# Block-wise weight conversions, a later half normalisation and a moved transpose in a fused attention and MoE kernel

## The chip, the cores and the metric

The kernel runs on one core of one Trainium2 chip. The metric is the device time of one execution in microseconds; the time of a kernel is the median of its runs. A core has TensorE (PE in the rows; PEld is its weight load), VectorE (DVE), ScalarE (ACT), GpSimd (POOL), and SyncE (SP), which in this kernel only issues transfers (DMAs). Each engine works through its own queue in order; an instruction that waits holds up all that is queued behind it on its engine.

## What is computed

The inputs are fp32. Attention with 2 x 8 heads, 768 tokens and 64 numbers a token is masked by clusters: a query sees the keys whose nearest of 16 centroids is the same. Two expert layers follow.

```python
def _attn_ref(q, k, v, centroids):
    ...
    q_assign = np.argmax(np.einsum('bhsd,hcd->bhsc', q_n, c_n), axis=-1)
    k_assign = np.argmax(np.einsum('bhsd,hcd->bhsc', k_n, c_n), axis=-1)
    mask = q_assign[:, :, :, None] == k_assign[:, :, None, :]
    scores = scale * np.matmul(q, k.transpose(0, 1, 3, 2))
    scores = np.where(mask, scores, -1000000000.0)
    ...
    return np.matmul(attn, v).astype(np.float32)

def _moe_ref(x, w_in, w_out):
    h = x @ w_in
    r = np.maximum(h, 0.0)
    return ((r * r) @ w_out).astype(np.float32)

def _moe2_ref(x, domain_probs, w1, w2):
    ...
    for e in range(E):
        h = np.maximum(x @ w1[e], 0.0)
        out += p[:, e:e + 1] * (h @ w2[e])
```

## The kernel before

All products run on fp32 numbers split in two parts, an upper one that TensorE's fp32r format holds and the rest (names with h and l: nkh, nkl, pth, ptl, w0h, w0l). The kernel has two stages. The attention stage takes the first quarter of the time; the two expert layers, a long row of products on TensorE, take the rest.

**Turns.** The attention stage is a loop over g = 0 to 95, one turn for each of 16 heads x 6 blocks of 128 queries. The work of a block is spread over turns. In turn g TensorE makes the scores S of block g + 2 (line 604, four products) and the transposes T of the exponentials of block g (line 637, six); VectorE makes the row maximum nb of block g + 2 (line 613); ScalarE the exponential p of block g + 1 (line 624); ScalarE and VectorE take T out of PSUM as pth (line 642) and ptl (line 643); the products with v (lines 651 and 653) follow for an earlier pair of blocks. The tables ORDER (one for even, one for odd turns) set in which order the code for a turn's steps is written, and so each engine's queue. A letter is a step: S, M (maximum), E (exponential), T0 and T1, P0 and P1 (products with v), O (taking their result out, line 675), and room for other work: X1 and X2 are two slots, each of which takes one function from the list `slots` for that turn, with its evacuation at Y1 or Y2; R runs the list `early`; C takes one step from the list dq; K is the place of the weight conversions.

**Pairs.** Heads go in pairs, 12 turns each. "Place p" below is turn g with g mod 12 = p. For the next pair of heads these steps are laid into a pair's turns:

- places 10, 11, 0, 1: the transposes of k and q (`trans_slot`, line 369, four slots). ScalarE takes each out as kqf (line 376), and GpSimd makes the upper parts nkh, nqh (line 52, `round_pool`) and the rests nkl, nql (line 378);
- places 1 and 2: the assignment scores (`pair_scores`, line 419), two halves, from nkh, nkl, nqh, nql; ScalarE copies them to ys (line 425);
- places 2 and 3: the scores are transposed back (`pair_turn`, line 435), two halves of three transposes; VectorE reduces each (line 440). All these steps share one PSUM buffer m;
- places 4 to 7: the one-hot rows. VectorE's maxima (lines 476, 480) and GpSimd's lines 465 to 473 are taken from dq; at place 7 TensorE transposes the result (`pair_hot`, line 492), and SyncE spreads it (`hot_rows`, line 509);
- `stack`: SyncE copies nkh, nkl, nqh, nql into the operands k1, q1, k2, q2 of the scores (lines 390, 392), for one head at places 1 and 3, for the other at places 8 and 9. GpSimd may write the next pair's nkh when these copies have landed.

Two more loads lie in these turns. `norm_steps` divides a finished pair's result by its row sums: the reciprocal (lines 707, 708) at place 3, its transpose (line 713) at place 4, a transfer through HBM that spreads it into rb (line 725) at place 5, a sum (line 734) at place 6, and then on GpSimd the two halves f5(0) and f5(1) at places 7 and 8: a product into rb (line 688), its upper part (line 52) and the rest (line 697), into xa. And `split64` converts the first layer's first weights, four blocks, which arrive as 64-bit words, to fp32: f1, f2, f4, f5, f6 on VectorE (lines 167, 170, 173, 178, 183), all in one buffer cva, then f3: ScalarE's copy w0h (line 189) and GpSimd's subtraction w0l (line 191), which reads cva last. They form one list cq of 24 steps; from turn 8 on a turn at places 6 to 10 takes one step, the blocks following each other without regard to the places. `load_piece` brings pieces of the next weights by SyncE, two at place 10 when the list is short enough.

Of the kernel before, what the change touches and what calls it, by code (L numbers as in the profile page):

```python
# [28 lines left out]
AT = {"stack1": (-11, -10), "stack": (-9, -9), "ohd": -7, "splitv": -3, "load": -10,  # L29
      "t": [-14, -13, -12, -11], "a": [-11, -10, -10, -9, -5], "conv": 8, "turns": (6, 7, 8, 9, 10)}  # L30


@with_exitstack
def moe_attention_kernel(
# [19 lines left out]
    B, H, S, D = q.shape  # L54
# [151 lines left out]
    with tc.manual_schedule():  # L206
# [175 lines left out]
        def stack(i, part):  # L382
            (kh, kl), (qh, ql) = kq[i // 2, "nk"], kq[i // 2, "nq"]
            r = slice(D * (i % 2), D * (i % 2) + D)
            for nm, rows, top, low in ((("k1", 128, kh, kl),),
                                       (("q1", 128, qh, qh), ("k2", D + C, kh, None),
                                        ("q2", D + C, ql, None)))[part]:
                t = stk[i, nm] = stk_p.tile(
                    [rows, S], F32R, tag=nm, name=nm, bufs=3 if nm == "k1" else 2)
                nc.sync.dma_start(out=t[0:D].bitcast(F32), in_=top[r].bitcast(F32))  # L390
                if low is not None:
                    nc.sync.dma_start(out=t[D:2 * D].bitcast(F32), in_=low[r].bitcast(F32))
# [307 lines left out]
        def norm_steps(hp):  # L700
# [38 lines left out]

            return [[f1], [], [f2], [f3], [f4], [lambda: f5(0)], [lambda: f5(1)]]  # L740

# [382 lines left out]
        for j in range(1, NH // 2):  # L1124
# [3 lines left out]
            for n, f in enumerate([pair_scores(j, 0), pair_scores(j, 1), pair_turn(j, 0),  # L1128
                                   pair_turn(j, 1), pair_hot(j)]):
                u = START["a"][n] if j == 1 else u0 + AT["a"][n]  # L1130
                if n == 4:
                    at(slots, u, lambda: None)
# [4 lines left out]
        for kk in range(KD):  # L1137
            at(early, 2 * NTT + kk, lambda kk=kk: load_in(kk))
        cq, lq = [], []
        for j in range(NF):  # L1140
            cq += [f for fs in split64(0, 0, j, cv_p[0]) for f in fs]
        for half in range(2):
            lq += [lambda half=half, n=n: load_piece(half, n) for n in range(4)]
        nq = []
# [5 lines left out]
        for g in range(NU):  # L1150
# [31 lines left out]
            def convert():  # L1182
                turn = g % (2 * NTT)
                if g >= AT["conv"] and cq and not dq and turn in AT["turns"]:
                    cq.pop(0)()
                if lq and turn == AT["turns"][-1] and len(cq) <= (12 if len(lq) > 4 else 0):
                    for _ in range(2):
                        lq.pop(0)()

# [202 lines left out]
```

## Time and profile before

| | |
|---|---|
| time of the kernel, median of 3 runs | 1040.4 us (1039.88 to 1041.51) |
| the profiled execution's own time | 1040.2 us |
| its span, first to last instruction | 1038.4 us |
| TensorE busy | 1016.5 us (98%) |
| VectorE, ScalarE, GpSimd busy | 676.1, 528.8, 567.5 us |

The profile is one execution, with a row for each instruction. Starts are counted from the first instruction. The granted clock is the share of TensorE's full 2.4 GHz. Idle time of an engine before an instruction is shown in square brackets with what ended it; an arrow in a wait reads "waited for".

### The profile page before, as it was taken

Reading aid. Unit: us, or ns where it says so; the run is one execution under the profiler, and the core shown is the slowest. Engines: PE = TensorE matmul, PEld = TensorE weight load, DVE = VectorE, ACT = ScalarE, POOL = GpSimd, SP = SyncE. Lnnn points to the kernel's source line nnn. Section 1 sums busy time; section 2 is a strip of 40 time slices with the busy share of each in tenths; the row PEclk is TensorE's granted clock in tenths of the full one; section 3 lists DMA queues with packets and bytes.
Section 4 is the critical chain, followed back from the end, with each engine's and each line's share of the span. In section 5 each row is a group of like instructions: output and inputs, shape, how many; then the busy total and the mean of one; then the engine's idle time right before and its main releaser. Section 6 shows DMA issues by size and latency. Waiting matters only on the chain.

```text
span 1038.4 us, 14897 instructions
## 1 busy us (share of the span) xinstructions
PE 1016.5 (98%) x5507; PEld 901.7 (87%) x5507; DVE 676.1 (65%) x1047; ACT 528.8 (51%) x1066; POOL 567.5 (55%) x557
## 2 busy tenths in 40 slices
PE   8998999999999999999999999999999999999998
PEld 7987888989888888888888998998988888898897
DVE  8887898879786773741175555577776555555654
ACT  7886887889755443434343333333444333333331
POOL 4465766665332222235456566567678566576650
PEclk9999999999999999999999999999999999999999
DMA  6576666665023230221012122122123121121101
GB/s 149 123 178 149 147 162 144 155 164 128 1 83 121 82 118 5 84 78 41 1 41 82 41 81 81 41 82 76 47 81 126 57 81 61 62 82 56 67 1 62
DMA packets 73745, 88.86 MB, mean 86 GB/s; under 512 B 27252, under 2 KB 50184, under 8 KB 73672
## 3 DMA queue, kind: packets, MB, share of 16 engines
q1 hardware_dynamic: 73672, 87.91, 29.8%
q8 instruction: 43, 0.70, 0.3%
q14 instruction: 30, 0.25, 0.1%
HBM read 62.58 MB, written 3.19 MB: 63 GB/s over the span
## 4 chain that ended last, share of the span: by engine, by line
PE 81%; DVE 3%; DMA 1%; SPq 1%; ACT 1%; POOL 1%; issue 1%; POOLq 0%; ACTq 0%
PE bank L965 25%; PE bank L925 22%; PE bank L818 13%; PE bank L794 4%; PE bank L793 4%; PE bank L795 4%; PE t L637 2%; PE s L604 2%; PE po L651 1%; PE po L653 1%; DVE ptl L643 1%; DVE nb L613 1%; PE m L419 1%; PE s L793 0%; DMA k<-nkh 0%
## 5 line engine op out<-in xcount | busy, mean ns | idle before, releaser
L965 PE MATMUL bank<-w1h,ga 128*128 128x512 f32 x768 | 269.9, 393 | 0.0
L975 DVE SCALAR_TENSOR_TENSOR x<-bank,pe_p,x 128x512 f32<-128x512 f32 x180 | 134.8, 750 | 167.5 <-PE bank L965 167.4
L925 PE MATMUL bank<-xa,w0h 128*128 128x384 f32 x896 | 228.2, 335 | 0.1
L925 PEld LDWEIGHTS bank<-xa,w0h 128*128 128x128 f32 x896 | 164.5, 188 | 17.9 <-ACT fa L936 0.5
L965 PEld LDWEIGHTS bank<-w1h,ga 128*128 128x128 f32 x768 | 144.1, 188 | 24.5
L804 POOL TENSOR_TENSOR ga<-fa,ga 128x512 fp32r<-128x512 f32 x48 | 63.2, 1317 | 178.0 <-ACT ga L803 137.0
L965 PE MATMUL bank<-w1l,ga 128*128 128x512 f32 x384 | 151.6, 395 | 0.0
L925 PE MATMUL bank<-xa,w0l 128*128 128x384 f32 x448 | 149.7, 334 | 0.0
L936 ACT COPY fa<-bank 128x384 f32<-128x384 f32 x96 | 45.6, 475 | 171.6 <-PE bank L925 171.6
L818 PE MATMUL bank<-ga,w1h 128*128 128x512 f32 x384 | 126.6, 389 | 0.0
L945 ACT ACTIVATE ga<-fa 128x384 fp32r<-128x384 f32 x96 | 50.5, 526 | 135.5 <-DVE fa L939 135.5
L894 POOL TENSOR_TENSOR w0l<-raw,w0h 128x512 fp32r<-128x512 f32 x64 | 75.0, 1195 | 81.2 <-ACT w0h L893 81.2
L912 POOL TENSOR_TENSOR w1l<-raw,w1h 128x1024 fp32r<-128x1024 f32 x32 | 77.2, 2414 | 71.3 <-ACT w1h L911 71.3
L643 DVE TENSOR_TENSOR ptl<-t,pth 128x384 fp32r<-128x384 f32 x192 | 97.7, 547 | 21.3 <-ACT pth L642 20.6
L613 DVE TENSOR_REDUCE nb<-s 128x1 f32<-128x768 f32 x96 | 91.2, 950 | 16.3 <-PE s L604 15.0
L637 PE MATMUL t<-identf,p 128*128 128x128 f32 x576 | 87.5, 279 | 7.7 <-DVE ptl L643 7.6
L624 ACT ACTIVATE p<-s,nb 128x768 f32<-128x768 f32 x96 | 88.0, 917 | 9.0 <-DVE nb L613 8.7
L642 ACT CAST pth<-t 128x384 fp32r<-128x384 f32 x192 | 84.0, 486 | 14.5 <-PE t L637 14.4
L948 DVE SCALAR_TENSOR_TENSOR ga<-fa,ga 128x384 fp32r<-128x384 f32 x96 | 90.1, 938 | 0.6 <-ACT ga L945 0.6
L604 PE MATMUL s<-k,q 80*128 80x384 f32 (+1 forms) x384 | 85.2, 343 | 0.5 <-DMA k<-ohm 0.3
L801 ACT ACTIVATE fa<-bank 128x512 f32<-128x512 f32 x44 | 26.4, 599 | 116.3 <-PE bank L795 116.3
L818 PEld LDWEIGHTS bank<-ga,w1h 128*128 128x128 f32 x384 | 72.0, 188 | 14.8
(213 smaller groups left out, 2051.9 us busy)
## 6 DMA issues: line engine op xcount, KB each, us to landing
raw<-in_moe_w_dram SPq DMA_DIRECT2D x64, 512.0 KB, 4.4
raw<-in_moe_w_in_dram SPq DMA_DIRECT2D x7, 1024.0 KB, 5.2
raw<-in_moe_w_out_dram SPq DMA_DIRECT2D x6, 1024.0 KB, 4.8
k<-nkh SPq DMA_DIRECT2D x28, 192.0 KB, 3.5
q<-nqh SPq DMA_DIRECT2D x28, 192.0 KB, 4.0
nv<-in_v_dram SPq DMA_DIRECT2D x16, 192.0 KB, 3.8
out_dram<-x SPq DMA_DIRECT2D x12, 256.0 KB, 2.1
k<-nkl SPq DMA_DIRECT2D x14, 192.0 KB, 3.3
```

Source lines behind the costliest of these rows:

```text
L604: nc.tensor.matmul(s[:, j, 0:HALF], stk[i, nq][:, t * 128:(t + 1) * 128], stk[i, nk][:, j * HALF:(j + 1) * HALF], start=first, stop=not first)
L613: nc.vector.tensor_reduce(out=nb, in_=s_ps[u][:, :, 0:HALF], axis=AX.XY, op=ALU.max, negate=True)
L624: nc.scalar.activation(p, s_ps.pop(u)[:, :, 0:HALF], AF.Exp, bias=nb_t.pop(u), accum_out=sums_t[hp][:, i % 2, t:t + 1])
L637: nc.tensor.transpose(tp[:, j], p_sb[u][:, half, j * 128:(j + 1) * 128], identf)
L642: return (lambda: nc.scalar.copy(dh, tp), lambda: nc.vector.tensor_tensor(dl, tp, dh.bitcast(F32), op=ALU.subtract))
L643: lambda: nc.vector.tensor_tensor(dl, tp, dh.bitcast(F32), op=ALU.subtract))
L818: nc.tensor.matmul(o, a, b, start=(ft == 0 and z == 0), stop=(ft == NF - 1 and z == 2))
L912: nc.gpsimd.tensor_tensor(lo, w, hi.bitcast(F32), op=ALU.subtract)
L925: nc.tensor.matmul(ps, w[:, o:o + 128], r_op(r, x)[:, kt], start=(first and kt == 0 and z == 0), stop=(kt == 1 and z == 2), skip_group_che ...
L948: nc.vector.scalar_tensor_tensor(out=g_t(n, f, t, 1), in0=h_src(n, f, t), scalar=0.0, in1=g_t(n, f, t, 0).bitcast(F32), op0=ALU.max, op1=A ...
L965: nc.tensor.matmul(o, a, w[:, f], start=(f == 0 and z == 0), stop=(f == 1 and z == 2))
L975: nc.vector.scalar_tensor_tensor(out=acc, in0=o, scalar=pc, in1=acc, op0=ALU.mult, op1=ALU.add)
```

## The change

Four things are laid out anew; no instruction is added or left out. The conversion steps get turns of their own: the first block 8, 9, 10, 18, 19 and, for f3, 27; block j = 1 to 3 the places 6 to 10 of one pair and place 3 of the next for f3 (turns 30 to 34 and 39, and so on). The load pieces stand at turns 46, 58, 70 and 82 (before: 34, 46, 70 and 82). f5(1) leaves place 8 and stands at place 2, in the next pair's turns; for the last but one pair it stays. The second `pair_turn` of each pair but the first goes to the second slot of its turn, behind the products with v. And `stack` copies k2 before q1.

```diff
--- before.py
+++ after.py
@@ -27,7 +27,7 @@
 WARM = [12, 10, 5, 11, 3, 9]
 START = {'t': [0, 0, 1, 1], 'a': [3, 3, 4, 4, 7], 'stack1': 4, 'stack': 5, 'head': 2}
 AT = {"stack1": (-11, -10), "stack": (-9, -9), "ohd": -7, "splitv": -3, "load": -10,
-      "t": [-14, -13, -12, -11], "a": [-11, -10, -10, -9, -5], "conv": 8, "turns": (6, 7, 8, 9, 10)}
+      "t": [-14, -13, -12, -11], "a": [-11, -10, -10, -9, -5], "conv": (8, 9, 10, 18, 19, 27), "pieces": 46, "second": 2}
 
 
 @with_exitstack
@@ -383,7 +383,7 @@
             (kh, kl), (qh, ql) = kq[i // 2, "nk"], kq[i // 2, "nq"]
             r = slice(D * (i % 2), D * (i % 2) + D)
             for nm, rows, top, low in ((("k1", 128, kh, kl),),
-                                       (("q1", 128, qh, qh), ("k2", D + C, kh, None),
+                                       (("k2", D + C, kh, None), ("q1", 128, qh, qh),
                                         ("q2", D + C, ql, None)))[part]:
                 t = stk[i, nm] = stk_p.tile(
                     [rows, S], F32R, tag=nm, name=nm, bufs=3 if nm == "k1" else 2)
@@ -737,7 +737,10 @@
             def f5(half):
                 norm_scaled(hp, half, st["rb"][:, half * HALF:(half + 1) * HALF], nc.gpsimd, round_pool)
 
-            return [[f1], [], [f2], [f3], [f4], [lambda: f5(0)], [lambda: f5(1)]]
+            if hp == NH // 2 - 2:
+                return [[f1], [], [f2], [f3], [f4], [lambda: f5(0)], [lambda: f5(1)]]
+            at(early, (2 * hp + 4) * NTT + AT["second"], lambda: f5(1))
+            return [[f1], [], [f2], [f3], [f4], [lambda: f5(0)]]
 
         def norm_last(hp):
             st = {}
@@ -1128,7 +1131,7 @@
             for n, f in enumerate([pair_scores(j, 0), pair_scores(j, 1), pair_turn(j, 0),
                                    pair_turn(j, 1), pair_hot(j)]):
                 u = START["a"][n] if j == 1 else u0 + AT["a"][n]
-                if n == 4:
+                if n == 4 or n == 3 and j > 1:
                     at(slots, u, lambda: None)
                 at(slots, u, f)
             if j + 1 < NH // 2:
@@ -1136,11 +1139,15 @@
         at(slots, START["head"], onehot_slot(1))
         for kk in range(KD):
             at(early, 2 * NTT + kk, lambda kk=kk: load_in(kk))
-        cq, lq = [], []
+        convs = {}
         for j in range(NF):
-            cq += [f for fs in split64(0, 0, j, cv_p[0]) for f in fs]
-        for half in range(2):
-            lq += [lambda half=half, n=n: load_piece(half, n) for n in range(4)]
+            steps = [f for fs in split64(0, 0, j, cv_p[0]) for f in fs]
+            b0 = (2 * j + 3) * NTT
+            turns = AT["conv"] if j == 0 else [b0 + x for x in (0, 1, 2, 3, 4, 9)]
+            for u, f in zip(turns, steps):
+                at(convs, u, f)
+        for n in range(8):
+            at(convs, AT["pieces"] + n // 2 * 2 * NTT, lambda n=n: load_piece(n // 4, n % 4))
         nq = []
 
         def early_gemm1(n):
@@ -1180,12 +1187,8 @@
                     f()
 
             def convert():
-                turn = g % (2 * NTT)
-                if g >= AT["conv"] and cq and not dq and turn in AT["turns"]:
-                    cq.pop(0)()
-                if lq and turn == AT["turns"][-1] and len(cq) <= (12 if len(lq) > 4 else 0):
-                    for _ in range(2):
-                        lq.pop(0)()
+                for f in convs.pop(g, []):
+                    f()
 
             def finish(n):
                 f = end.pop(n, None)
```

How the queues change, at three places. GpSimd, from the end of f5(0) on, in the turns 45 to 51 (nk and nq are the next pair's k and q, vv the split of v). Before:

```order
L688 TENSOR_TENSOR rb<-rb,xs 128x384
L52 TENSOR_SCALAR xa<-rb 128x128
L697 TENSOR_TENSOR xa<-rb,xa 128x128
L52 TENSOR_SCALAR xa<-rb 128x256
L697 TENSOR_TENSOR xa<-rb,xa 128x256
L52 TENSOR_SCALAR vv<-nv 128x6x64
L310 TENSOR_TENSOR vv<-nv,vv 128x6x64
L52 TENSOR_SCALAR nkh<-kqf 128x384
L378 TENSOR_TENSOR nkl<-kqf,nkh 128x384
L191 TENSOR_TENSOR w0l<-cva,w0h 128x4x128
L52 TENSOR_SCALAR nkh<-kqf 128x384
L378 TENSOR_TENSOR nkl<-kqf,nkh 128x384
```

After, from the last rounding of q on; the rows from vv to this one now follow f5(0) directly:

```order
L52 TENSOR_SCALAR nqh<-kqf 128x384
L378 TENSOR_TENSOR nql<-kqf,nqh 128x384
L688 TENSOR_TENSOR rb<-rb,xs 128x384
L52 TENSOR_SCALAR xa<-rb 128x128
L697 TENSOR_TENSOR xa<-rb,xa 128x128
L52 TENSOR_SCALAR xa<-rb 128x256
L697 TENSOR_TENSOR xa<-rb,xa 128x256
L52 TENSOR_SCALAR vv<-nv 128x6x64
L310 TENSOR_TENSOR vv<-nv,vv 128x6x64
L191 TENSOR_TENSOR w0l<-cva,w0h 128x4x128
```

The five rows of f5(1) stood ahead of the rounding of k and q and now stand behind it; line 191 stood between two of the roundings and now follows all of them.

VectorE at places 2 to 4 of the pair from turn 12 on. Before:

```order
L440 TENSOR_REDUCE A<-m 128x192
L613 TENSOR_REDUCE nb<-s 128x1
L440 TENSOR_REDUCE A<-m 128x192
L707 TENSOR_SCALAR r<-sums 128x12
L643 TENSOR_TENSOR ptl<-t,pth 128x3x128
L708 RECIPROCAL r<-r 128x12
L643 TENSOR_TENSOR ptl<-t,pth 128x3x128
L613 TENSOR_REDUCE nb<-s 128x1
L476 TENSOR_REDUCE mx<-A 128x24
```

After:

```order
L440 TENSOR_REDUCE A<-m 128x192
L613 TENSOR_REDUCE nb<-s 128x1
L707 TENSOR_SCALAR r<-sums 128x12
L643 TENSOR_TENSOR ptl<-t,pth 128x3x128
L708 RECIPROCAL r<-r 128x12
L643 TENSOR_TENSOR ptl<-t,pth 128x3x128
L440 TENSOR_REDUCE A<-m 128x192
L613 TENSOR_REDUCE nb<-s 128x1
L476 TENSOR_REDUCE mx<-A 128x24
```

The second reduction (line 440) moved from ahead of the reciprocal and of both ptl to behind them, just ahead of the next row maximum.

SyncE, the copies into the score operands of one head (k_762 is k1; k_808 before and k_805 after are k2; q_805 before and q_807 after are q1; q_810 is q2). Before:

```order
L390 DMA k_762<-nkh 64x768
L392 DMA k_762<-nkl 64x768
L390 DMA q_805<-nqh 64x768
L392 DMA q_805<-nqh 64x768
L390 DMA k_808<-nkh 64x768
L390 DMA q_810<-nql 64x768
```

After:

```order
L390 DMA k_762<-nkh 64x768
L392 DMA k_762<-nkl 64x768
L390 DMA k_805<-nkh 64x768
L390 DMA q_807<-nqh 64x768
L392 DMA q_807<-nqh 64x768
L390 DMA q_810<-nql 64x768
```

The copy into k2, the last one that reads nkh, moved ahead of the two copies into q1.

## Rows read from the trace of the kernel before

**Rows 1.** The page: the chain of work that ended last, by engine.

```profile
PE 81%; DVE 3%; DMA 1%; SPq 1%; ACT 1%; POOL 1%; issue 1%; POOLq 0%; ACTq 0%
```

**Rows 2.** Stretches: us; busy PE, PEld, DVE, ACT, POOL; granted clock; DMA share; GB/s.

```profile
42.05:59.18 17.13, 16.16 (x121) 15.06 (x120) 12.52 (x22) 14.16 (x35) 7.49 (x10) 1.00 0.70 169
73.17:95.33 22.16, 17.30 (x121) 16.38 (x120) 13.65 (x22) 14.92 (x36) 15.80 (x21) 0.92 0.50 113
109.35:127.67 18.32, 16.47 (x122) 14.85 (x120) 13.61 (x22) 15.04 (x36) 15.55 (x21) 1.00 0.68 157
141.68:162.37 20.69, 18.18 (x122) 16.43 (x120) 13.88 (x23) 15.35 (x37) 16.14 (x21) 0.92 0.67 158
176.01:193.23 17.22, 16.25 (x122) 14.91 (x120) 14.49 (x23) 14.37 (x35) 14.21 (x20) 1.00 0.63 139
207.22:224.40 17.18, 16.21 (x122) 15.08 (x120) 11.71 (x19) 14.19 (x35) 14.39 (x21) 1.00 0.72 169
207.22:216.74 9.52, 9.52 (x76) 9.07 (x75) 7.64 (x12) 8.91 (x23) 7.39 (x12) 1.00 0.76 162
89.18:95.33 6.15, 6.15 (x48) 6.05 (x47) 4.06 (x7) 5.29 (x14) 4.34 (x6) 1.00 0.18 35
```

**Rows 3.** Waits, 20 to 290 us: total us, times, longest us.

```profile
DVE cva L167 <- POOL w0l L191: 6.9, 2, 5.4
...
PE m L419 <- POOL nqh L52: 2.2, 3, 1.6
...
POOL A L465 <- DVE mx L476: 39.6, 7, 6.9
```

**Rows 4.** Timeline of pass 2: start, us, engine, line, operation, [idle before].

```profile
77.58 1.02 POOL L688 TENSOR_TENSOR rb<-rb,xs 128x384 f32<-128x384 f32 x1
...
80.66 1.26 POOL L191 TENSOR_TENSOR w0l<-cva,w0h 128x512 fp32r<-128x512 f32 x1
...
81.96 0.72 DVE L167 TENSOR_SCALAR cva<-raw 128x512 int32<-128x512 int32 x1 [5.36 <-POOL w0l L191]
...
84.06 1.54 PE L637 MATMUL t<-identf,p 128*128 128x128 f32 x6 [4.51 <-DVE ptl L643]
```

**Rows 5.** Timelines, line 183 beside GpSimd; line 189: ns min/median/max.

```profile
145.48 0.67 DVE L183 SCALAR_TENSOR_TENSOR cva<-raw,cva 128x512 int32<-128x512 int32 x1
...
182.35 1.42 DVE L183 SCALAR_TENSOR_TENSOR cva<-raw,cva 128x512 int32<-128x512 int32 x1
...
182.22 1.01 POOL L310 TENSOR_TENSOR vv<-nv,vv 128x384 fp32r<-128x384 f32 x1
...
L189 ACT CAST w0h<-cva x10: 614/632/661, 73.5 to 423.9; 128x512 fp32r<-128x512 f32 x10
```

**Rows 6.** Timeline of pass 4, SyncE (SPq), GpSimd; last: us to landing.

```profile
144.90 0.57 SPq L390 DMA_DIRECT2D q<-nqh  x1
...
146.51 0.87 SPq L390 DMA_DIRECT2D k<-nkh  x1
...
151.44 0.51 POOL L52 TENSOR_SCALAR nkh<-kqf 128x384 fp32r<-128x384 f32 x1 [1.81 <-ACT p L624]
...
k<-nkh SPq DMA_DIRECT2D x2, 192.0 KB, 4.7
```

**Rows 7.** Place 3 (turn 39) as a stretch; timeline of turns 39 to 41.

```profile
127.67:130.76 3.09, 2.70 (x22) 2.38 (x21) 3.02 (x7) 1.88 (x5) 0.00 (x0) 1.00 1.01 240
...
128.41 0.55 DVE L440 TENSOR_REDUCE A<-m 128x192 f32<-128x384 f32 x1
...
129.00 0.31 PEld L435 LDWEIGHTS m<-identf,ys 128*128 128x128 f32 x3 [0.71 <-DVE A L440]
...
131.68 0.96 DVE L613 TENSOR_REDUCE nb<-s 128x1 f32<-128x768 f32 x1
...
133.01 1.01 DVE L643 TENSOR_TENSOR ptl<-t,pth 128x384 fp32r<-128x384 f32 x2
...
133.65 0.97 PE L637 MATMUL t<-identf,p 128*128 128x128 f32 x6
```

## The prediction

> **What bounds the kernel now.** I read the chain of work that ended last first: TensorE carries 81% of it, the other engines a few per cent in all [rows 1]. From 286 us on that is TensorE without a gap, and the change does not reach there. So the question is how much TensorE loses in the attention stage, and I cut that stage by turns, whose starts are the first score product on line 604 of each. A pair of heads is 12 turns; I write "place 9" for the tenth turn of a pair. The work for the next pair (its transposes, its assignment scores) lies at places 10, 11, 0, 1 and 2, so I took the stretches of places 9 to 2. There are six; I call them passes 1 to 6, in order of time. Two undisturbed pieces give the length that TensorE needs: places 9 to 0 of pass 6, 9.52 us, and places 1 and 2 of pass 2, 6.15 us. In both TensorE is busy all the time, so 15.67 us is the floor. Against it the six passes are too long by 1.46, 6.49, 2.65, 5.02, 1.55 and 1.51 us, together 18.7 us [rows 2]. That is all that this change can take from these stretches.
>
> The list of waits of the attention stage says what ends them [rows 3]: VectorE's first conversion step (line 167, writing cva) waited 6.9 us in two places for GpSimd's line 191, the last reader of cva; TensorE's assignment scores (line 419) waited 2.2 us in three places for GpSimd's rounding of q (line 52). GpSimd itself stood idle 39.6 us in seven places before line 465. It is late in one part of the pair and idle in another.
>
> **The conversions.** The timeline of pass 2 shows the largest loss whole [rows 4]. GpSimd starts the second half of the normalisation (line 688) at 77.58, comes to line 191 at 80.66 and leaves it at 81.92; VectorE, which had taken up line 167 of the next block, has stood 5.36 us; the row maximum and the exponential behind it are late, and TensorE idles 4.51 us before its transposes. What is queued behind line 167 on VectorE is thus every turn's work. TensorE's clock falls with it: passes 2 and 4, in which TensorE is idle longest (4.9 and 2.5 us), have a mean granted clock of 0.92, so for a part of them the lower of its two levels, 1.2 instead of 2.4 GHz; the other four have 1.00 [rows 2]. This loss is inside the 6.49 and 5.02 us and goes with the idling.
>
> After the change a block's five VectorE steps stand at places 6 to 10 and the ScalarE copy with line 191 at place 3 behind them, three turns (over 6 us) ahead of the next block's line 167. That wait has no place left. What stays is VectorE's own load: five steps in five turns. Pass 5 has exactly this layout today (turns 54 to 58), so its 1.55 us is the upper bound for passes 3, 4 and 5; the lower is 0, pass 6, which has no steps. In between: pass 5's last step (line 183) took 1.42 us, since GpSimd was in line 310; not held up, it took 0.67 in pass 4 [rows 5]. With the second half of the normalisation gone from there, GpSimd runs line 310 some 2.9 us earlier, is through with it and waits for a DMA when that step comes. I take 0.75 us off and leave 0.8 us in each of passes 3, 4 and 5, and 0.5 in pass 2, where only two of the block's steps (turns 18 and 19) precede. The copy on ScalarE (line 189) stands at the end of place 3, where ScalarE is busy 1.88 of 3.09 us [rows 7]: nothing. If that cover were gone it would cost its own length, 0.63 us [rows 5], four times.
>
> That GpSimd and VectorE block each other is also what the Trainium skill states ("SBUF — State Buffer", Who interferes with whom): a VectorE instruction in a 2-port mode, or with two SBUF inputs, and a GpSimd instruction hold a shared port pair in turn. By that rule the moved GpSimd work could hit VectorE at places 2 and 3; this is the third rival below.
>
> **The half normalisation.** In each pair 2.9 us of GpSimd work (77.58 to 80.7 in pass 2, [rows 4]) leave the queue ahead of the rounding of k and q and go behind it, to place 2. Five or three instructions move; they issue no DMA. In passes 2 to 6 the rounding is ready earlier. Behind them now wait the value split and line 191, and then line 465. The idle time before line 465 is 39.6/7 = 5.7 us a pair; 2.9 + 1.3 us of moved work leave 1.5 us. So I cost it at nothing. The transfer that reads the normalised buffer's successor (rb, line 725) is issued at place 5, and ScalarE's first copy into the same xs buffer comes at the end of place 3, a full turn after the place where line 688 reads it.
>
> **k2 first on SyncE's queue.** GpSimd may overwrite nkh only when its last reader, the transfer into k2 (line 390), has landed. In pass 4 that one was issued at 146.51, two transfers after 144.90, and GpSimd began at 151.44, when it had landed (4.7 us) [rows 6]. Now it is issued in the place of the first q1 transfer, 1.6 us earlier. Passes 1 and 6 are too long by 1.46 and 1.51 us and wait for nothing else, so both go to 0; in passes 3 to 5 it helps too. Bounds: 0 to 1.6 us a pass. q1 lands later by one transfer; its reader is seven turns away.
>
> The Trainium skill says that completion on such a queue is not in order of issue ("DMA: Bandwidth & Descriptors", Queues, rings and completion order). By that k2 could land as late as now, and the sum would be that of the second rival. The row, 4.7 us from issue to landing, does not decide it alone.
>
> Pass by pass the excess after is then 0, 0.5, 0.8, 0.8, 0.8 and 0: 2.9 us of 18.7 stay, **15.8 us go**.
>
> **The second transposes back.** At place 3 the three transposes of line 435 waited for VectorE to clear the one buffer m, and TensorE stood 0.71 us before their weight load [rows 7]. Behind the products of the turn they wait for nothing. So six pairs could gain up to 6 x 0.7 = 4.3 us. But VectorE has no slack: from 128.41 it works without a break to the row maximum at 131.68, which waits 0.2 us, and then to the two line 643 at 133.01; TensorE's transposes, which write into what the first of them has read, start at 133.65 [rows 7]. TensorE that comes 0.7 us earlier meets the same VectorE, and gains the 0.2 us. It can lose too: the reciprocal's transpose (line 713) in the next turn uses m, and now waits for line 440, so below nothing by one line 440, 0.55 us, or -3.3 us. Between -3.3 and 4.3 I take 0.2 x 6 less 0.4 us that turn 51 loses because it no longer profits from the stall before it: **0.8 us**.
>
> The load pieces move to turns 46, 58, 70 and 82, the last two as now; what they bring is converted only after the attention stage. Nothing.
>
> **Sum.** Own time of the profiled execution 1040.2 us (span 1038.4 and 1.8 around it; the median of the three runs is 1040.4). 1040.2 - 15.8 - 0.8 = **1023.6 us**.
>
> **Rivals.** (1) The transposes give their full 0.7 us, because VectorE's chain is shorter than I think: 0.8 becomes 4.3, **1020.1 us**. For it: TensorE's wait there is real; against it: VectorE's unbroken row of work. (2) The k2 transfer lands no earlier, or GpSimd is late anyway: passes 1, 4 and 6 keep 1.5 us each, **1028.1 us**. For it: transfers there crowd (DMA share 0.67 to 0.72 in those stretches, [rows 2]); against: the start at 151.44 follows the landing at once. (3) The moved GpSimd work blocks VectorE's small SBUF steps at place 3 (lines 707 and 708): up to one GpSimd instruction, 1.0 us, in each of six pairs, and the 0.8 us are lost: **1030.4 us**. Against it: line 707 ran in places with an idle GpSimd, so no row shows it; and by my order of events GpSimd is at that moment waiting for line 189. (4) On the other side: GpSimd becomes late for the one-hot rows, which it makes in lines 465 to 473 and which TensorE transposes at place 7 (line 492). It decides from the point where the moved work ends more than 1.5 us later than I reckon; each further us is then one of TensorE's in each of six pairs, since all of its later work is queued behind line 492. Slower by 0.2% needs a loss of 16.6 + 2.1 us, with a little over it 3.2 us a pair, so a GpSimd that is 4.7 us late: the moved 4.2 us would have to take twice as long. That gives 1023.6 + 6 x 3.2 = **1042.8 us**. (5) All goes back into VectorE's load and nothing is left, within 0.2% (about what a measurement of this kernel can tell from no change): the 5.36 us wait cannot come back, so this is very unlikely.
>
> **How the numbers follow.** Forecast 0.72, rivals (1) 0.09, (2) 0.09, (3) 0.06, (4) 0.02, (5) 0.02. The range takes in (1) and (2), and the bounds of VectorE's load, 3 x 0.75 us up, 3 x 0.8 and 0.5 down: 1019.0 to 1029.0 us. Faster 0.96, same 0.02, slower 0.02.
>
> **What will show it.** In the changed profile: no wait of line 167 for line 191; no wait of line 419 for GpSimd; granted clock 1.00 in all six passes; each pass between 15.6 and 16.5 us; line 435 without idle time, place 3 shorter but places 4 and 5 longer by most of it; GpSimd's idle time before line 465 down to 1 or 2 us a pair. I would be wrong if line 465 no longer waits for VectorE, if GpSimd's first nkh still begins some 5 us after the q1 issue, or if passes 3 and 4 stay above 17 us.

## The result, and the profile after

The changed kernel takes 1025.9 us (median of 4 runs, 1025.34 to 1028.38) against 1040.14 for the kernel before beside it (4 runs): a ratio of 0.9866, with a 95% interval of 0.9847 to 0.9884. Forecast were 1023.6 us and a range of 1019.0 to 1029.0. The profiled execution took 1025.7 us (span 1023.7; before 1040.2 and 1038.4). The slowest of the four runs, 1028.38 us, had a mean granted clock of 0.998 over its span, the other three 0.999 to 1.000.

The chain of work that ended last [rows 1] can't be compared. In the kernel before it is followed back only to 119.7 us, in the changed kernel to 0.7 us, so TensorE's 81% there and 86% here are shares of different stretches.

The six passes, cut as in [rows 2] (stretch; us; busy PE, PEld, DVE, ACT, POOL; granted clock; DMA share; GB/s):

```profile
43.08:58.75 15.67, 15.67 (x122) 15.14 (x120) 12.54 (x22) 14.17 (x35) 7.47 (x10) 1.00 0.69 163
72.36:89.85 17.49, 16.03 (x122) 15.05 (x120) 12.31 (x20) 14.31 (x35) 11.95 (x17) 1.00 0.69 159
103.82:120.09 16.27, 15.89 (x121) 14.98 (x120) 13.17 (x23) 14.23 (x35) 12.11 (x17) 1.00 0.66 144
134.27:150.62 16.35, 16.29 (x122) 14.89 (x120) 13.79 (x23) 14.28 (x35) 11.50 (x16) 1.00 0.75 178
164.86:180.53 15.67, 15.67 (x121) 14.99 (x120) 13.12 (x23) 14.21 (x35) 12.54 (x18) 1.00 0.76 179
194.22:210.15 15.93, 15.91 (x122) 15.08 (x120) 11.71 (x19) 14.24 (x35) 12.27 (x18) 1.00 0.71 170
```

Over the floor of 15.67 us they are too long by 0, 1.82, 0.60, 0.68, 0 and 0.26 us, together 3.4. Forecast were 0, 0.5, 0.8, 0.8, 0.8 and 0, together 2.9. The granted clock is 1.00 in all six. So the passes gave 15.3 us where 15.8 were forecast, and one of them, the second, is off by 1.3 us.

Places 3 to 5, where the moved transposes lie, are to be read pair by pair (turns 15 to 17, 27 to 29, and so on; same columns):

```profile
58.75:65.85 7.10, 7.04 (x55) 6.51 (x54) 7.10 (x15) 5.96 (x15) 1.83 (x3) 1.00 1.09 224
89.85:97.31 7.46, 7.04 (x55) 6.48 (x54) 7.46 (x15) 6.49 (x16) 5.49 (x8) 1.00 1.02 231
120.09:127.76 7.67, 7.21 (x55) 6.45 (x54) 7.67 (x15) 6.49 (x16) 5.71 (x9) 1.00 0.93 215
150.62:158.37 7.75, 7.26 (x56) 6.45 (x54) 7.75 (x15) 6.49 (x16) 5.78 (x9) 1.00 1.09 235
180.53:187.71 7.18, 7.04 (x55) 6.49 (x54) 7.18 (x15) 6.43 (x16) 5.29 (x7) 1.00 1.16 221
210.15:217.25 7.10, 7.04 (x55) 6.52 (x54) 7.10 (x15) 5.96 (x15) 3.91 (x6) 1.00 0.95 223
```

Before, these stretches took 7.49, 7.51, 7.51, 7.13, 7.49 and 7.51 us (from the same starts of line 604). VectorE is busy for the whole of each, as [rows 7] had it. The first and the last pair fell to 7.10 us; of the four between, two fell (7.18 and 7.46) and two are longer than before (7.67 and 7.75). In all it is 0.4 us, forecast 0.8.

The list of waits of the attention stage (20 to 290 us; total us, times, longest) answers [rows 3]:

```profile
POOL A L465 <- DVE mx L476: 15.3, 7, 5.8
POOL rb L688 <- DMA rb<-rd: 15.0, 6, 4.5
...
PEld m L713 <- DVE A L440: 3.0, 6, 0.7
...
PE s L604 <- DMA k<-ohm: 1.5, 2, 1.1
...
PE m L713 <- DVE A L440: 1.3, 3, 0.5
```

Line 167's wait for line 191 (6.9 us before) and TensorE's line 419 waiting for line 52 (2.2) are gone from the list. GpSimd's idle time before line 465 fell from 39.6 to 15.3 us. TensorE's wait of line 604 for the one-hot rows (k<-ohm) grew from 0.3 us in one place to 1.5 in two, and its wait of line 713 for line 440 is new.

### The profile page after: what moved, and what is told of

Read it like the earlier page. It is cut to its first block, busy times and chain, and to the rows that moved or that the text cites. A ratio compares the mean times of both kernels' runs of the same rounds, so it can differ in the third digit from the quotient of the medians.

```text
span 1023.7 us, 14890 instructions
## 1 busy us (share of the span) xinstructions
PE 1012.1 (99%) x5507; PEld 900.0 (88%) x5507; DVE 674.7 (66%) x1047; ACT 528.7 (52%) x1066; POOL 565.9 (55%) x557
## 4 chain that ended last, share of the span: by engine, by line
PE 86%; DVE 6%; POOL 2%; DMA 2%; SPq 1%; issue 1%; ACT 1%; DVEq 0%; POOLq 0%; ACTq 0%
PE bank L968 26%; PE bank L928 22%; PE bank L821 13%; PE bank L798 4%; PE bank L797 4%; PE bank L796 4%; PE t L637 4%; PE s L604 4%; PE po L651 2%; DVE ptl L643 2%; PE po L653 2%; DVE nb L613 1%; PE m L419 1%; DVE A L440 1%; PE m L369 1%
## 5 line engine op out<-in xcount | busy, mean ns | idle before, releaser
L643 DVE TENSOR_TENSOR ptl<-t,pth 128x384 fp32r<-128x384 f32 x192 | 97.7, 547 | 20.0 <-ACT pth L642 19.8
```

What stands on the lines that cost most here:

```text
L643: lambda: nc.vector.tensor_tensor(dl, tp, dh.bitcast(F32), op=ALU.subtract))
```

## The experiments

A name with u_ is the changed kernel with one part undone, o_ the kernel before with only the part named, x_ the changed kernel with a further edit. Each was cut as the two above; the tables give the excess of the six passes over 15.67 us and the length of places 3 to 5, pair by pair, in its profiled execution. Times are medians, ratios are against the kernel before, run on the same chip beside it (its medians were 1039.5 to 1040.3). The intervals reach about 1 to 2 us either way, so a difference of some 2 us or less between two kernels rests on the stretches and not on the times alone.

In these executions TensorE's mean granted clock was 1.00 in every pass but these: passes 2 and 4 of the kernel before, pass 2 of u_conv and of u_half, pass 4 of o_half, passes 2, 3 and 4 of o_turn (0.92 in each), and pass 2 of o_k2 (0.80) and of o_k2load (0.85). In these passes a part of the excess is TensorE's own work at the lower of its two levels.

### One part taken out of the changed kernel

| kernel | us | ratio, interval | passes 1 to 6: excess | places 3 to 5 |
|---|---|---|---|---|
| before | 1040.1 | 1 | 1.46 6.49 2.65 5.02 1.55 1.51 | 7.49 7.51 7.51 7.13 7.49 7.51 |
| after | 1025.9 | 0.9866, 0.9847 to 0.9884 | 0.00 1.82 0.60 0.68 0.00 0.26 | 7.10 7.46 7.67 7.75 7.18 7.10 |
| u_conv | 1029.0 | 0.9897, 0.9884 to 0.9911 | -0.02 5.77 0.67 1.05 0.08 -0.03 | 7.10 7.10 7.67 7.55 7.18 7.10 |
| u_half | 1028.9 | 0.9898, 0.9883 to 0.9913 | -0.03 4.60 1.20 1.11 1.34 1.22 | 7.11 7.11 7.10 7.10 7.10 7.11 |
| u_k2 | 1033.1 | 0.9944, 0.9932 to 0.9957 | 1.49 1.38 2.47 1.72 1.48 1.50 | 7.10 7.76 7.75 7.75 7.75 7.33 |
| u_turn | 1027.8 | 0.9887, 0.9874 to 0.9901 | -0.02 1.87 0.56 0.60 0.65 0.01 | 7.51 7.85 7.84 7.84 7.83 7.51 |

u_conv lays conversions and load pieces out as before:

```diff
-                for f in convs.pop(g, []):
-                    f()
+                turn = g % (2 * NTT)
+                if g >= AT["conv"] and cq and not dq and turn in AT["turns"]:
+                    cq.pop(0)()
...
```

> The changed kernel with the conversions and load pieces laid out as before, the other three parts kept. Theory (each part's gain as in the forecast): line 167 waits for line 191 again, but with the half normalisation gone from GpSimd's queue only 2 to 3 us in pass 2 instead of 5.4, so about 1025.9 + 2.5 = 1028.5 us. Rival: the conversion layout carries nearly all of the gain by itself; then pass 2 is again 22 us long and the time is 1032 us or more.

It costs 3.1 us, nearly all of it in pass 2, where line 167 waits for line 191 again:

```profile
DVE cva L167 <- POOL w0l L191: 4.3, 1, 4.3
```

TensorE idles 2.06 us behind it, and with the clock at 0.92 its busy time in the pass is 17.88 us against 16.03 in the changed kernel. So this wait is the conversions' part, as predicted. The other passes hardly change: once GpSimd is early there, line 191 is not late.

u_half puts f5(1) back ahead of the roundings:

```diff
-            if hp == NH // 2 - 2:
-                return [[f1], [], [f2], [f3], [f4], [lambda: f5(0)], [lambda: f5(1)]]
-            at(early, (2 * hp + 4) * NTT + AT["second"], lambda: f5(1))
-            return [[f1], [], [f2], [f3], [f4], [lambda: f5(0)]]
+            return [[f1], [], [f2], [f3], [f4], [lambda: f5(0)], [lambda: f5(1)]]
```

> The changed kernel with the second half of the normalisation back at place 8, the other three parts kept. Theory: GpSimd's rounding is late again, so line 419 waits for GpSimd about 1.4 us in pass 2 and up to 0.5 us in passes 5 and 6, and line 183 meets a busy GpSimd again (0.75 us in passes 3 to 5); against that line 707 is no longer held up at place 3 (0.16 us instead of up to 0.8). Together 1027 to 1029 us. Rival: GpSimd's move cost as much as it gave, since lines 707 and 713 pay for it; then 1025.9 us within 1 us.

The time is 3.0 us up, as expected. The passes lose 6.1 us and places 3 to 5 gain 1.6: all six pairs are at 7.10 or 7.11. What holds pairs 2 to 5 above that in the changed kernel is thus the moved half of the normalisation, which the prediction had costed at nothing. The ScalarE copy (line 189) stands at place 3 in this kernel too and costs nothing there.

Of the 6.1 us, 2.8 lie in pass 2, and they are not shown to be the half normalisation's. TensorE waits longer for the one-hot rows there (2.14 us, 1.11 in the changed kernel), and the clock falls to 0.92 (busy time 17.78 us against 16.03):

```profile
77.02 0.58 PE L604 MATMUL s<-k,q 80*128 80x384 f32 x2 [2.14 <-DMA k<-ohm]
```

SyncE issues these rows behind rb, and rb came 4.32 us after rd in this execution, 2.60 in that of the changed kernel, although SyncE's queue up to there is the same in both. In passes 3 to 5 VectorE's line 178 takes 1.26 to 1.27 us each time (changed kernel: 0.78, 1.28 and 0.77); line 183, which the expectation named, takes 0.72 or 0.73.

u_k2 copies q1 ahead of k2 again:

```diff
-                                       (("k2", D + C, kh, None), ("q1", 128, qh, qh),
+                                       (("q1", 128, qh, qh), ("k2", D + C, kh, None),
```

> The changed kernel with q1 copied before k2 as before, the other three parts kept. Theory: nkh is free 1.6 to 2 us later in every pair, passes 1 and 6 are 1.5 us longer and line 419 waits for GpSimd, in passes 3 to 5 by less: 1029 to 1031 us. Rival: transfers land out of order and the place in the queue does not matter: 1025.9 us within 1 us, passes 1 and 6 as short as now.

This is the part with the highest price, 7.2 us, above either expectation: 1.0 to 1.9 us in every pass but the second, not in passes 1 and 6 alone, and places 3 to 5 at 7.75 in four pairs (all of GpSimd's later work is late with it). The copy into k2 of pass 4, ScalarE's copy into kqf and GpSimd's first rounding of k, in this kernel and, second, in the changed one:

```profile
141.76 0.88 SPq L390 DMA_DIRECT2D k<-nkh  x1
...
143.49 0.48 ACT L376 ACTIVATE kqf<-m 128x384 f32<-128x384 f32 x1
...
146.22 0.52 POOL L52 TENSOR_SCALAR nkh<-kqf 128x384 fp32r<-128x384 f32 x1 [5.13 <-ACT p L624]
```

```profile
137.47 0.57 SPq L390 DMA_DIRECT2D k<-nkh  x1
...
140.78 0.48 ACT L376 ACTIVATE kqf<-m 128x384 f32<-128x384 f32 x1
...
142.47 0.51 POOL L52 TENSOR_SCALAR nkh<-kqf 128x384 fp32r<-128x384 f32 x1 [4.09 <-ACT xo L675]
```

In both the rounding starts 4.5 to 5.0 us after the k2 issue, as in [rows 6] (the engines named as releasers were long done). Counted from the start of the pass (136.95 and 134.27) it starts at 9.27 and at 8.20 us: 1.1 us earlier, for a transfer issued 1.6 us earlier. The landing of this transfer is in neither trace; by the start of the rounding behind it, the place in the queue matters.

u_turn puts the second transposes back into the first slot:

```diff
-                if n == 4 or n == 3 and j > 1:
+                if n == 4:
```

> The changed kernel with the second transposes back in the first slot again, the other three parts kept. Theory (VectorE sets the pace of places 3 to 5): place 3 is 3.1 us again and place 4 2.2, so a pair loses 0.4 us at most: 1025.9 to 1027.5 us. Rival (TensorE's wait at place 3 was real time): 6 x 0.7 us more, 1030 us.

1.9 us, between the two expectations, and 2.1 at places 3 to 5 (46.38 less 44.26 us for the six pairs). By time alone the two kernels are hardly told apart (the intervals of their ratios overlap); the stretches show it. It is two and a half times the 0.8 of the sum, and between the bounds of -3.3 and 4.3.

### One part alone in the kernel before

| kernel | us | ratio, interval | passes 1 to 6: excess | places 3 to 5 |
|---|---|---|---|---|
| o_conv | 1033.3 | 0.9934, 0.9921 to 0.9947 | 1.49 1.38 2.57 1.65 1.47 1.57 | 7.49 7.80 7.78 7.78 7.78 7.49 |
| o_half | 1035.6 | 0.9960, 0.9946 to 0.9974 | 1.51 1.61 2.12 4.54 1.54 1.53 | 7.49 7.49 7.50 7.14 7.48 7.49 |
| o_k2 | 1037.4 | 0.9975, 0.9966 to 0.9985 | -0.01 10.43 2.89 2.39 0.33 -0.01 | 7.51 7.51 7.51 7.49 7.49 7.49 |
| o_turn | 1040.4 | 1.0002, 0.9992 to 1.0011 | 1.51 6.12 4.71 4.41 1.51 1.53 | 7.10 7.10 7.10 6.90 7.10 7.10 |
| o_k2load | 1034.3 | 0.9945, 0.9931 to 0.9958 | -0.03 6.57 3.10 2.18 0.40 -0.03 | 7.52 7.52 7.51 7.50 7.50 7.52 |

The edits of the first four are those above the other way round, applied to the kernel before.

> The kernel before with the conversions and load pieces laid out as in the changed kernel, nothing else of the change. Taking this part alone out of the changed kernel cost about 3 us (pass 2 was 5.8 us over its floor instead of 1.8, all else nearly as before). Theory A, the parts take different losses and add up: alone it brings about 3 us, in pass 2, 1037. Theory B, that of the prediction: all that lies behind the wait of line 167 for line 191 is this part's, 4.5 us of idle TensorE in pass 2 and the clock behind it, and the same in pass 4: 7 to 9 us, 1031 to 1033, with passes 1, 5 and 6 still 1.5 us too long.

6.3 us: between the two theories, nearer to B. Passes 2 and 4 lose 5.1 and 3.4 us of their excess, 8.5 together, and every pass but the third (2.57) is left with about 1.5 us, the price of the late k2. The clock is 1.00 in all passes: 3.2 of the 8.5 us are TensorE's busy time in these two, 35.5 us before and 32.3 here. Places 3 to 5 give 1.5 us back: here ScalarE's copy (line 189), put at the end of place 3, is not hidden. The exponential behind it is late, and with it pth, ptl and TensorE's transposes. GpSimd waits for it as well, since it is idle there:

```profile
126.71 0.62 ACT L189 CAST w0h<-cva 128x512 fp32r<-128x512 f32 x1
...
127.23 0.91 ACT L624 ACTIVATE p<-s,nb 128x768 f32<-128x768 f32 x1
127.38 0.49 PE L637 MATMUL t<-identf,p 128*128 128x128 f32 x3
127.41 1.29 POOL L191 TENSOR_TENSOR w0l<-cva,w0h 128x512 fp32r<-128x512 f32 x1 [4.49 <-ACT w0h L189]
...
129.37 0.31 PEld L637 LDWEIGHTS t<-identf,p 128*128 128x128 f32 x3 [0.40 <-DVE ptl L643]
```

> The kernel before with only the second half of the normalisation moved to place 2 of the next pair. Theory A: GpSimd is 2.9 us earlier at line 191, so the 5.4 us wait of line 167 shrinks to about 2.5 and pass 2 loses 2 to 3 us less; passes 3 to 5 gain little since k2 is still late; places 3 to 5 become about 0.3 us longer in each of three pairs, because line 707 (0.16 us) is held up beside GpSimd: 2 to 4 us in all, 1036 to 1038. Theory B, costed at nothing as in the prediction: places 3 to 5 stay at 7.5 us and line 707 at 0.16.

4.0 us, the upper end of theory A. Line 167 waits 1.7 us in one place, pass 2 is down to 1.61 with its clock at 1.00, and places 3 to 5 don't move: theory A in the passes, B at the places. Line 707 takes at most 0.37 us here: it meets only the end of line 310.

> The kernel before with only k2 copied ahead of q1. Taking this part alone out of the changed kernel cost 7 us: 1.5 us in passes 1, 5 and 6 each, 1 to 1.9 in passes 3 and 4. Theory A, the copy into k2 sets the start of the rounding in every pass: passes 1, 5 and 6 fall to 0 to 0.2 and the sum is 4.5 to 7 us, 1033 to 1035.5. Theory B, that of the prediction's sum: only passes 1 and 6 wait for nothing else, 3 us, 1037.

2.2 us, less than either theory. Passes 1, 4, 5 and 6 gain 6.8 us, as theory A has it (its 1.5 us per pass), but pass 2 loses 3.9. The stretch of that pass, the list of waits and the timeline show the way; SPq is SyncE's queue:

```profile
72.48:98.58 26.10, 20.22 (x122) 18.88 (x120) 13.65 (x22) 14.92 (x36) 15.76 (x21) 0.80 0.46 106
```

```profile
DVE cva L167 <- POOL w0l L191: 9.8, 2, 8.2
```

```profile
66.29 0.95 SPq L129 DMA_DIRECT2D raw<-in_moe_w_in_dram  x1
...
68.37 0.41 SPq L719 DMA_DIRECT2D rd<-rt  x1
...
72.86 1.11 SPq L725 DMA_DIRECT2D rb<-rd  x2
...
77.09 0.99 POOL L688 TENSOR_TENSOR rb<-rb,xs 128x384 f32<-128x384 f32 x1 [5.33 <-DMA rb<-rd]
...
77.75 0.98 PE L604 MATMUL s<-k,q 80*128 80x384 f32 x2 [1.98 <-DMA k<-ohm]
```

The attention's turns come 1.5 us earlier and the transfers ahead of rd do not (the load at 66.29 was at 65.38 before, in an execution whose turn 0 began 0.76 us sooner). rb is issued 4.5 us after rd (6 KB), GpSimd stands 5.33 us, and line 191 behind it makes line 167 wait 8.2 us. TensorE waits twice in this pass: 1.98 us for the one-hot rows, which are issued behind rb, and 3.56 us for line 643 behind line 167. In the kernel before it waited 4.51 us in the second place alone. The clock is 0.80 for 0.92 there, and TensorE's busy time 20.22 us for 17.30: 2.9 of the 3.9 us are the lower clock.

> The kernel before with only the second transposes back moved behind the products of their turn. Theory A: TensorE regains 0.4 us in places 3 to 5 of each of five pairs (7.5 to 7.1 us; the pair at turn 51 is at 7.1 already), 2 us, 1038. Theory B, the prediction's size: 0.2 us a pair less 0.4, 0.8 us, 1039.4. Rival of its lower bound: line 713 waits for line 440 and it is slower, up to 3 us.

No change (0.9992 to 1.0011), although places 3 to 5 fall by 2.2 us in all. In this execution pass 3 is 2.1 us longer: line 167 waits 2.57 us there for line 191, before 1.55, TensorE idles 2.25 us behind it, before 1.22, and the clock, 1.00 in this pass before, is 0.92:

```profile
108.75:129.13 20.38, 17.86 (x122) 16.38 (x120) 13.21 (x22) 15.02 (x36) 15.96 (x21) 0.92 0.60 142
```

TensorE's busy time is 1.4 us up (16.47 before), its idle time 0.7. It was not this execution alone: over their whole spans 5 of the 11 runs of o_turn had a mean granted clock of 0.995, and 1 of the 22 runs of the kernel before beside it. So what the transposes gain is here lost again at the next late GpSimd, and for the most part by the clock.

o_k2load moves the loads of line 129 as well, to turns in which SyncE is idle:

```diff
-            at(early, 2 * NTT + kk, lambda kk=kk: load_in(kk))
+            at(early, 5 + kk // 2, lambda kk=kk: load_in(kk))
```

> The kernel before with k2 ahead of q1 and, as the second edit, the four 64-bit weight loads at turns 5 and 6 instead of 12 to 15. With k2 first alone, passes 1, 4, 5 and 6 gained 6.8 us and pass 2 lost 3.9 (10.4 us over the floor), which left 2.2 us for the whole kernel. Theory A: pass 1 ends 1.5 us earlier and meets the same backlog of transfers, in which the loads stand; rd and rb land late, GpSimd comes late to line 191, and line 167 waits 8.2 us. With the loads out of the way pass 2 is back at 5 to 6.5 us and all is 4 us less than with k2 first alone: 1033. Theory B: the backlog is that of the attention's own transfers (k, q, v, q1, q2): pass 2 stays near 10 us, 1037.

3.0 us less than with k2 first alone, where theory A had 4, and pass 2 is back at 6.57. rd is issued 3.7 us earlier than with the loads in their old place and rb 4.8, and TensorE does not wait for the one-hot rows. The same transfers now:

```profile
64.63 0.95 SPq L719 DMA_DIRECT2D rd<-rt  x1
68.07 1.59 SPq L725 DMA_DIRECT2D rb<-rd  x2
72.69 1.01 POOL L688 TENSOR_TENSOR rb<-rb,xs 128x384 f32<-128x384 f32 x1 [1.02 <-DMA rb<-rd]
```

The moved loads alone in the kernel before were not run.

The parts do not add up one by one. Alone they bring 6.3, 4.0, 2.2 and 0 us, 12.5 together; taken out they cost 3.1, 3.0, 7.2 and 1.9, 15.2 together; the whole brings 14.2. These totals are no further apart than the noise allows, but the shares are: 6.3 against 3.1 for the conversions, 2.2 against 7.2 for k2. Conversions and half normalisation both shorten the one wait for line 191, so either has a large part of it alone. k2 and the transposes show their worth only where that wait is gone.

### What is left: two edits to the changed kernel

| kernel | us | ratio, interval | passes 1 to 6: excess | places 3 to 5 |
|---|---|---|---|---|
| x_no | 1025.3 | 0.9854, 0.9839 to 0.9870 | -0.02 2.09 0.40 1.05 0.75 -0.03 | 7.02 7.02 7.02 7.04 7.02 7.02 |
| x_load | 1023.2 | 0.9838, 0.9824 to 0.9851 | -0.01 0.48 0.22 0.52 0.80 -0.01 | 7.11 7.09 7.67 7.80 7.11 7.10 |
| x_both | 1021.8 | 0.9824, 0.9811 to 0.9838 | -0.03 0.49 0.43 0.55 0.82 -0.01 | 7.03 7.03 7.02 7.03 7.03 7.03 |

What line 707 does at place 3 of the changed kernel (turn 39), and behind it:

```profile
121.86 1.01 POOL L310 TENSOR_TENSOR vv<-nv,vv 128x384 fp32r<-128x384 f32 x1
122.16 0.73 DVE L707 TENSOR_SCALAR r<-sums 128x12 f32<-128x12 f32 x1
...
122.81 0.54 DVE L643 TENSOR_TENSOR ptl<-t,pth 128x384 fp32r<-128x384 f32 x1
...
123.82 0.54 DVE L440 TENSOR_REDUCE A<-m 128x192 f32<-128x384 f32 x1
...
124.41 0.27 PE L713 MATMUL m<-identf,r 128*12 128x128 f32 x1 [0.46 <-DVE A L440]
```

Twelve numbers a partition take 0.73 us instead of 0.16, and end 0.02 us after GpSimd's line 310. In the pairs of turns 27 and 51 it is the same (0.53 and 0.80 us, both ending within 0.03 us of line 310's end). Ptl, line 440 and TensorE's line 713 come late behind it. u_half, in which GpSimd is idle there, and u_k2, in which all four pairs meet it, bracket the case (count; ns least, median, most):

```profile
L707 DVE TENSOR_SCALAR r<-sums x7: 160/161/161, 60.1 to 239.8; 128x12 f32<-128x12 f32 x7
```

```profile
L707 DVE TENSOR_SCALAR r<-sums x7: 161/814/824, 61.7 to 243.4; 128x12 f32<-128x12 f32 x7
```

x_no leaves out line 707, the addition of 1e-9 to the row sums:

```diff
-                    lambda: nc.vector.tensor_scalar(r, sm, 1e-9, None, op0=ALU.add),
-                    lambda: nc.vector.reciprocal(r, r),
+                    lambda: None,
+                    lambda: nc.vector.reciprocal(r, sm),
```

> The changed kernel without VectorE's line 707 (in the stage of turns): it leaves out the addition of 1e-9 to the row sums, and line 708 takes the reciprocal of the sums themselves. Theory A: what the moved half of the normalisation costs at places 3 to 5 is line 707 standing up to 0.8 us beside GpSimd; without it the pairs at turns 27, 39 and 51 fall from 7.46, 7.67 and 7.75 us to 7.10 to 7.25, as with the half normalisation at its old place, 1.2 to 1.6 us in all, 1024.3. Theory B: another small step of VectorE (line 708, or 440) is held up in its place, or the 0.4 us belong to line 440 and line 713: places 3 to 5 stay at 7.4 to 7.8, same time as the changed kernel (1025.9).

All six pairs are at 7.02 to 7.04 us, so 2.1 us of stretch go (44.26 to 42.14), and line 708 keeps its 0.21 us with GpSimd's line 310 beside it (theory A). Pass by pass and place by place 1.2 us go; the median falls by 0.6 us and the runs spread from 1023.0 to 1026.6: by time alone the edit is not told from the changed kernel. Passes 2, 4 and 5 of this execution are 1.4 us longer together, pass 2 by TensorE's wait for k<-ohm (1.37 us).

x_load moves the loads of line 129, with the diff of o_k2load. The hot rows of turn 22 in the changed kernel and, second, in x_load (turn 22 starts at 75.13 and at 74.40):

```profile
69.19 0.40 SPq L719 DMA_DIRECT2D rd<-rt  x1
...
71.79 1.11 SPq L725 DMA_DIRECT2D rb<-rd  x2
...
72.99 0.66 SPq L509 DMA_DIRECT2D q<-ohm  x1
73.70 1.26 SPq L509 DMA_DIRECT2D k<-ohm  x2
...
76.76 0.59 PE L604 MATMUL s<-k,q 80*128 80x384 f32 x2 [1.11 <-DMA k<-ohm]
```

```profile
64.18 0.87 SPq L719 DMA_DIRECT2D rd<-rt  x1
68.24 1.11 SPq L725 DMA_DIRECT2D rb<-rd  x2
70.18 0.66 SPq L509 DMA_DIRECT2D q<-ohm  x1
70.89 1.26 SPq L509 DMA_DIRECT2D k<-ohm  x2
```

> The changed kernel with the four 64-bit weight loads (line 129) issued at turns 5 and 6, where SyncE is idle for 6 us, instead of turns 12 to 15. Theory A: they delay the transfers of the first pair, and with them the hot rows for turn 22; without them TensorE's wait of 1.11 us for k<-ohm goes, and pass 2 falls from 1.8 to 0.5 to 0.7 us over its floor, as predicted for the changed kernel: 1.1 to 1.3 us, 1024.7. Theory B: the hot rows wait in SyncE's queue behind rb, which waits for rd, whatever else is loaded: pass 2 stays at 1.8, no change; or pass 1 is disturbed by the earlier loads and it is slower.

Theory A: pass 2 falls from 1.82 to 0.48, the 0.5 that the prediction had for it, and TensorE does not wait for k<-ohm. The time is 2.7 us less than that of the changed kernel; by the stretches it is 1.7, and turn 0 began 0.7 us sooner.

> Both edits in one: no line 707 (the addition of 1e-9 is left out), and the four loads at turns 5 and 6. If the two losses are independent 2.4 to 2.9 us less than the changed kernel, 1023.2; if both theories fail, 1025.9.

1021.8 us, the fastest of all: 0.9824 of the kernel before, and 4.1 us less than the changed kernel. By the stretches 3.2 us go. What is left is 2.3 us in passes 2 to 5, in which VectorE has its conversion steps.

## Why the prediction was right, and where it was off

**The floor and the passes** held. 18.7 us could be had, 15.3 were. The wait of line 167 and that of line 419 are gone, the clock is 1.00 in all six passes. Passes 1 and 6 fell to 0 and 0.26. That the excess left, 3.4 us, came so near the 2.9 is in part luck: passes 3 to 5 came out 1.1 us better than reckoned and pass 2 1.3 us worse. That the loss by the clock goes with the idling is borne out: where the idling came back in part, as in u_conv and o_k2, the clock fell again. The 81% of the opening is the share of a chain that begins at 119.7 us; nothing in the sum uses it.

**Conversions:** right in mechanism. Passes 3 to 5 keep 0.60, 0.68 and 0 us (forecast 0.8 each), but 0.38 of the 0.60 are TensorE's wait for the one-hot rows at turn 34. Line 183 takes 0.68 us in all three, as reckoned, once GpSimd is through with line 310. In pass 4 line 310 met line 178 instead, which took 1.28 us beside it, against 0.78 and 0.77 in passes 3 and 5:

```profile
137.65 1.28 DVE L178 SCALAR_TENSOR_TENSOR cva<-raw,cva 128x512 int32<-128x512 int32 x1
```

Which step it meets differs from kernel to kernel.

**Pass 2** is the term that was mis-sized: 1.82 for 0.5. The 1.11 us before turn 22 are TensorE's wait for the one-hot rows, which the sum has no term for; with them the pass takes 17.49 us, outside the 15.6 to 16.5 that the prediction gave as a sign. The step that failed is "q1 lands later by one transfer; its reader is seven turns away": no other transfer was followed past the one moved. By k2 first the turns of the first pair come 1.5 us earlier, and meet a row of transfers, with the four loads in it, that the lateness had hidden. u_k2, where k2 is late again, has no such wait in pass 2, and x_load, where the loads stand elsewhere, has none either; o_k2load shows the same in the kernel before.

**k2 first:** right, and larger than reckoned. The sum gave it passes 1 and 6, 3.0 us, "in passes 3 to 5 it helps too". Without it the changed kernel is 7.2 us slower. The excess of passes 3 to 5 was laid to VectorE's steps, with pass 5 as the witness. But o_conv leaves 1.4 to 1.7 us in every pass but the third, whatever VectorE does there, and with k2 first in the kernel before pass 5 falls to 0.33: 1.2 of pass 5's 1.55 us were the late k2, too. Rival (2) did not happen; the rounding starts 1.1 us earlier. It would have cost 7 us, not 4.5. By the Trainium skill ("DMA: Bandwidth & Descriptors", Queues, rings and completion order) completion need not follow the order of issue; in these runs the instruction that waits for the moved transfer came 1.1 us earlier for an issue 1.6 us earlier.

**The transposes and the half normalisation:** the sum of 0.8 us came out at 0.4. That it came so near is luck: two errors nearly cancel. "TensorE that comes 0.7 us earlier meets the same VectorE" failed: with the half normalisation at its old place the changed kernel has 7.10 us in all six pairs, 2.0 us less than before in all (44.64 to 42.63), in spite of the ScalarE copy. Where the transposes stand as before, in o_conv, the copy costs 0.3 us in each of three pairs, half of the 0.63 that the prediction gave for a lost cover; the fourth is 0.65 us longer, as it no longer has the stall before it. And "I cost it at nothing" failed: at places 3 to 5 the moved work takes 1.6 us back. That is rival (3), in three pairs instead of six; its counter-argument, "GpSimd is at that moment waiting for line 189", was wrong by 0.7 us: in turn 39 line 707 starts at 122.16, and GpSimd begins to wait after 122.87. Line 713 waits 0.46 us for line 440, which the lower bound had foreseen, but only since line 707 pushed it: in x_no that product does not wait. The rest was as forecast: line 435 has no wait, place 3 of turn 39 fell from 3.09 to 2.42 us, and place 4 took it back.

**The cover of the copy** (line 189 costed at nothing) held in the changed kernel and fails without the moved transposes.

**Where the 2.1 us are** between 1023.6 and the profiled 1025.7: 0.5 in the passes, 0.4 at places 3 to 5, and 1.1 before turn 0, which began at 19.93 us against 18.83. By the other kernels, this last is not the change's: in one execution each of the other twelve, turn 0 began at 19.2 to 19.8 us, also in o_turn (19.36), which changes nothing ahead of it.

Rivals (1), (4) and (5) did not happen: places 3 to 5 gave 0.4 us, not 4.3, TensorE does not wait for the one-hot rows to be made, and GpSimd is still early for line 465.

## What to carry to other kernels

Before an excess is laid to a busy engine, look whether the same number stands in a stretch without that load: 1.5 us in passes 1, 5 and 6 alike was for the most part one cause, the last reader of a buffer standing third in a DMA queue. A step that pulls a stage forward is worth what the next thing behind it allows; follow every queue of the stage, loads for later stages included, by the amount of the gain. And when work moves to an idle engine, list the small instructions of the neighbour engine that it will now stand beside, since here a step of 0.16 us took up to 0.82. When a part brings nothing alone, look at the granted clock of its stretches before its mechanism is given up: o_turn gained 2.2 us at its own place and lost most of it in a pass whose clock fell.

## What the runs showed of the hardware

VectorE's tensor-scalar step of 128x12 fp32 numbers from SBUF to SBUF took 0.16 us beside an idle GpSimd and up to 0.82 beside GpSimd's line 310; in nine cases (four of the changed kernel, five of u_k2) it ended 0.02 to 0.04 us after GpSimd's instruction. The reciprocal of the same numbers kept 0.21 us beside the same instruction (x_no, 122.01 to 122.22, line 310 from 121.25 to 122.26). The Trainium skill ("SBUF — State Buffer", Who interferes with whom) states that a VectorE instruction in a 2-port mode and a GpSimd instruction exclude each other, and that the one issued second is fully blocked for the whole of the other. The rows agree in that line 707 ended with GpSimd's instruction. They differ in that the 0.02 to 0.04 us behind GpSimd's end are less than its own 0.16, so by the rows a part of it was done before. No run here shows the port, or in which mode line 707 ran.

A 6 KB transfer (rd) stands in SyncE's queue behind larger ones, and the next transfer (rb) waits for it. With the four loads moved away, rd of the first pair was issued 3.7 us earlier (o_k2load against o_k2) and 5.0 us earlier (x_load against the changed kernel). From the issue of rd to that of rb it took 4.5 us with the loads in front and 3.4 without in the first two, but 2.6 with them and 4.1 without in the other two. With the same queue in front it was 2.6 us in the changed kernel and 4.3 in u_half. What sets this time the runs don't show.
